# Longformer attention and a softplus feed-forward on one core: the first two batches rounded in GpSimd's transfers, and a new order

## The chip, the core and the metric

The kernel runs on one core of a Trainium2 chip. Its engines are TensorE (PE: matmuls, with weight loads shown apart as PEld), VectorE (DVE), ScalarE (ACT), GpSimd (POOL) and SyncE (SP, which here only issues transfers). Each works through its own list of instructions in order and waits on semaphores for the others. Transfers run on 16 DMA engines and are asked for by SP, POOL or ACT. The metric is the device time of one execution in microseconds.

## The reference

```python
def _attn_ref(q, k, v, global_idx):          # q, k, v: 8 x 8 x 576 x 64, float32
    scores = scale * np.matmul(q, k.transpose(0, 1, 3, 2))
    mask = np.abs(pos[:, None] - pos[None, :]) <= 32
    mask = mask | is_global[:, None] | is_global[None, :]      # 8 global tokens
    scores = np.where(mask, scores, -1e9)
    attn = softmax(scores)
    return np.matmul(attn, v)

x = attn_out.transpose(0, 2, 1, 3).reshape(4608, 512)
h = x @ w_in                                  # 512 x 2048
g = np.maximum(h, 0.0) + np.log1p(np.exp(-np.abs(h)))
return g @ w_out                              # 2048 x 512
```

So eight batches of eight heads are attended to in a window of 32 tokens on each side and eight global tokens, and every token then passes a feed-forward layer with a softplus.

## The kernel before

**Tiles.** The 576 tokens of a batch are 18 blocks of 32. A "pair" is four blocks in a row, for all eight heads; there are 36 pairs, and four pairs make a tile of 512 tokens for the feed-forward part, nine in all. A pair goes through: scores s on PE; mask, maximum m, subtraction, exponentials on ACT, sum, reciprocal rs and normalization to pn; a transposition to pt on DVE; the values xo on PE; an eviction to xT. A tile then has 64 h matmuls of 512 columns (w_in), 16 softplus evaluations on ACT (L1292) and 64 o matmuls (w_out). The first two tiles are cut into pieces of pairs (one, two, one; then one, three), so that h can begin when the first pair is through.

**First batches.** For the first two batches q and k are loaded with tokens on partitions (L512), in parts: two of 256 tokens and a short one of 64. A part is rounded to bf16 (`cast`, L837; q is scaled there), PE transposes it and picks the global tokens out of it (`tr`, L845), and the result is evicted to qx and kx (`trev`, L870). `fill` copies the global keys into kx and `gev` the global queries into qg, when all parts of k or of q are through. The global tokens' own rows come from `sg` (scores of qg against all keys), a maximum, exponentials pg, a transposition pgt, `ov` on PE, and the scaled result vg, which the first tile's values need. Later batches are loaded by blocks (L460) and rounded on POOL or ACT.

**Weights and queues.** SP loads q and k; POOL asks for v of the first batch, for w_in (four quarters, each of three transfers, L1347) and for w_out, since those transfers round on the way. `follow` (L753) is a copy of two elements on SP that reads a weight: it stops SP until the weight has landed. So the second batch's q and k follow w_in's third quarter, and its v follows w_out's first.

**Order.** All work is entered as jobs with costs in ns, dependencies and buffers (`_Order`, L19). A table of numbers, ORDER (L359), says which job comes next and on which engine; a number is five times the job's number plus the engine. Where the planner sees PE wait, it puts in fill matmuls on idle data (L729), a share FILL of the pause; its results are not used. The costs and the transfers' queues (`settle`, L110) are the planner's own estimates.

## Time and profile before

| | |
|---|---|
| median of 3 runs | 332.98 us (332.73 to 333.11) |
| the profiled execution | 333.06 us |
| its span, first to last instruction | 331.4 us |
| PE busy | 317.9 us, 96% of the span |
| ACT, DVE, POOL busy | 231.7, 220.9 and 193.3 us |
| granted TensorE clock | 0.999 |

An engine's busy time is the time in which it works on an instruction. A timeline row gives the start, the length, the engine, the line, the operation, out<-in, the shape and the number of instructions, and in brackets how long the engine was idle before it and what released it. Releasers are inferred: of several, the last to come by the profile is named. The term "issue" means that nothing in the profile explains the pause.

### The profile page before, as it was taken

The numbers are of one execution on the slowest core, as the hardware profiler recorded it, in microseconds if no ns is written. First come the engines' busy times: TensorE is split into PE (matmuls) and PEld (weight loads), VectorE is DVE, ScalarE is ACT, GpSimd is POOL, SyncE is SP. The second block draws the span as 40 slices with busy tenths as digits, with TensorE's granted clock in tenths as the row PEclk, the third lists the DMA queues.
The fourth block names the chain that finished last, engine by engine and source line by source line (L and its number), as shares of the span: only waits on it lengthen the run. The fifth ranks groups of instructions, "written<-read, shape, count | busy, mean of one in ns | idle before, by whom it ended". The sixth has DMA issues, their size and how long they took to land.

```text
span 331.4 us, 12080 instructions
## 1 busy us (share of the span) xinstructions
PE 317.9 (96%) x5281; PEld 168.8 (51%) x5281; DVE 220.9 (67%) x387; ACT 231.7 (70%) x460; POOL 193.3 (58%) x173
## 2 busy tenths in 40 slices
PE   8778998899999999999999999999999999999995
PEld 3537874576555444544454445445544454454453
DVE  7697578786995999993895498819966890440000
ACT  5799759696897678489778947866457467925712
POOL 7865654994783596878648675496327764420000
PEclk9999999999999999999999999999999999999999
DMA  7999899898878998996994759650001112000102
GB/s 192 185 201 223 166 201 177 139 184 187 154 122 156 169 209 157 203 227 112 157 188 75 179 135 143 150 168 3 4 0 65 36 65 95 2 34 32 65 16 112
DMA packets 168860, 42.14 MB, mean 127 GB/s; under 512 B 153320, under 2 KB 165864, under 8 KB 168808
## 3 DMA queue, kind: packets, MB, share of 16 engines
q1 hardware_dynamic: 155928, 27.15, 46.0%
q0 software_dynamic: 11008, 11.08, 17.0%
q10 hardware_dynamic: 1872, 3.15, 2.5%
q8 instruction: 41, 0.67, 0.9%
q14 instruction: 11, 0.09, 0.1%
HBM read 36.71 MB, written 9.44 MB: 139 GB/s over the span
## 4 chain that ended last, share of the span: by engine, by line
PE 71%; SPq 11%; DMA 9%; ACT 4%; issue 1%; POOL 1%; DVE 1%; POOLq 0%
PE o L1297 32%; PE h L1286 29%; SPq L464 5%; PE xo L1251 4%; DMA stage<-in_q_dram 4%; SPq L469 3%; PE s L1077 3%; DMA stage<-in_k_dram 3%; ACT st L1113 2%; DMA wout<-in_moe_w_out_dram 2%; PE ov L997 1%; DMA stage<-in_v_dram 1%; SPq L518 1%; PE pick L886 1%; SPq L514 1%
## 5 line engine op out<-in xcount | busy, mean ns | idle before, releaser
L1297 PE MATMUL o<-wout,g 128*128 128x512 bf16 (+1 forms) x592 | 138.6, 374 | 0.2 <-ACT g L1292 0.2
L1286 PE MATMUL h<-xT,win 128*128 128x512 bf16 (+3 forms) x768 | 136.7, 326 | 0.8 <-DMA win<-in_moe_w_in_dram 0.8
L1292 ACT ACTIVATE g<-h 128x512 bf16<-128x512 f32 (+3 forms) x192 | 83.9, 503 | 35.0 <-PE h L1286 33.4
L1286 PEld LDWEIGHTS <-win 128*128 128x128 bf16 x768 | 66.7, 98 | 59.7 <-issue 1.1
L1132 POOL TENSOR_TENSOR pn<-st,rs 128x1024 bf16<-128x1024 f32 (+1 forms) x36 | 64.7, 1806 | 42.9 <-DVE rs L1126 38.8
L1297 PEld LDWEIGHTS <-g 128*128 128x128 bf16 x592 | 55.5, 98 | 60.6 <-ACT g L1292 1.4
L1100 POOL TENSOR_TENSOR st<-st,m 128x1024 f32<-128x1024 f32 x32 | 60.5, 1899 | 28.3 <-DVE m L1094 28.2
L1124 DVE TENSOR_REDUCE sm<-st 128x8 f32<-128x1024 f32 x32 | 38.4, 1200 | 19.0 <-ACT st L1117 18.8
L1081 DVE TENSOR_TENSOR st<-s,mask 128x512 f32<-128x512 f32 x64 | 41.3, 678 | 9.3 <-PE s L1077 9.2
L1094 DVE TENSOR_REDUCE m<-st 128x8 f32<-128x1024 f32 x32 | 38.4, 1206 | 0.4
L1117 ACT ACTIVATE st<-st 128x1024 f32<-128x1024 f32 x32 | 32.7, 1051 | 3.2 <-POOL st L1100 3.0
L1141 DVE STREAM_TRANSPOSE pt<-pn 128x512 int32<-128x512 int32 x36 | 24.6, 693 | 10.4 <-POOL pn L1132 10.2
L720 ACT COPY osb<-o 128x512 f32<-128x512 f32 (+1 forms) x27 | 15.5, 575 | 20.3 <-PE o L1297 18.7
L720 ACT CAST xT<-xo 128x512 bf16<-128x512 f32 (+3 forms) x28 | 11.5, 474 | 14.5 <-PE xo L1251 14.5
L720 POOL CAST kb<-stage 128x1152 bf16<-128x1152 f32 (+2 forms) x9 | 11.5, 1273 | 10.8 <-DMA stage<-in_q_dram 8.8
L717 POOL TENSOR_SCALAR qb<-stage 128x1152 bf16<-128x1152 f32 (+1 forms) x11 | 12.9, 1177 | 8.1 <-DMA stage<-in_q_dram 6.5
L1292 ACT ACT_TABLE_LOAD x13 | 16.7, 1283 | 0.2
L1077 PE MATMUL s<-kx,qx 64*32 64x128 bf16 x1152 | 14.7, 220 | 1.3 <-issue 0.6
L720 DVE CAST xT<-xo 128x512 bf16<-128x512 f32 (+3 forms) x20 | 11.0, 582 | 6.5 <-PE xo L1251 6.5
L1077 PEld LDWEIGHTS <-qx 64*32 64x32 bf16 x1152 | 10.0, 90 | 10.3 <-issue 7.7
L720 POOL CAST vb<-stage 128x1152 bf16<-128x1152 f32 x9 | 10.3, 1150 | 6.8 <-DVE sm L1124 3.3
L1117 ACT ACT_TABLE_LOAD x11 | 14.1, 1283 | 0.2
(129 smaller groups left out, 301.6 us busy)
## 6 DMA issues: line engine op xcount, KB each, us to landing
stage<-in_v_dram SPq DMA_DIRECT2D x56, 144.0 KB, 4.2
stage<-in_k_dram SPq DMA_DIRECT2D x48, 144.0 KB, 4.1
stage<-in_q_dram SPq DMA_DIRECT2D x48, 144.0 KB, 3.5
out_dram<-osb POOLq DMA_DIRECT2D x24, 256.0 KB, 3.6
out_dram<-osb ACTq DMA_DIRECT2D x11, 256.0 KB, 2.0
stage<-in_q_dram SPq DMA_DIRECT2D x4, 512.0 KB, 6.5
stage<-in_k_dram SPq DMA_DIRECT2D x4, 512.0 KB, 7.4
wout<-in_moe_w_out_dram POOLq DMA_DIRECT2D x4, 512.0 KB, 7.8
```

What stands on the lines that cost most here:

```text
L720: {"ACT": nc.scalar.copy, "DVE": V.tensor_copy, "POOL": nc.gpsimd.tensor_copy}[e](out, in_)
L1077: nc.tensor.matmul(out=PS["s", n, g][quad(a), x, :], lhsT=qx[b % 2][rows(g), a, j * BL:(j + 1) * BL], rhs=kx[b % 2][rows(g), a, e0 * BL:(e ...
L1081: V.tensor_tensor(out=PS["st", n][:, h, :, :], in0=PS["s", n, h][:, :, :], in1=mask[:, h, j0:j0 + PB, :, :].rearrange("p j s i -> p j (s i ...
L1094: V.reduce_max(out=m[:], in_=flat(PS["st", n], h0, h1), axis=AX)
L1100: on(e).tensor_tensor(out=t, in0=t, in1=over(PS["m", n, y][:], SL * BL), op=OP.subtract)
L1117: nc.scalar.activation(out=t, in_=t, func=AF.Exp)
L1124: V.reduce_sum(out=sm[:], in_=flat(PS["st", n], h0, h1), axis=AX)
L1132: on(e).tensor_tensor(out=PS["pn", n][:, :, :, h0:h1].rearrange("p x s h -> p h x s"), in0=PS["st", n][:, h0:h1], in1=PS["rs", n, y][:].re ...
L1141: V.transpose(out=bass.AP(base.tensor, base.offset, ap=[list(base.ap[0]), [2 * STEP, PB // 2], [STEP + BL // 2, 2], [1, SL * BL]]), in_=PS ...
L1286: nc.tensor.matmul(out=h[:, :], lhsT=w_in_t[c // 4][:, kd, c % 4 * P:(c % 4 + 1) * P], rhs=PS["xT", m][:, kd, lo:hi], start=(kd == 0), sto ...
L1292: nc.scalar.activation(out=PS["g", m, c][:, lo:hi], in_=PS[key][:, lo_of(c, hi - lo)], func=AF.Softplus)
L1297: nc.tensor.matmul(out=PS["o", m, ns, a][:, :], lhsT=PS["g", m, kf][:, ns * P:(ns + 1) * P], rhs=w_out_t[kf // 4][:, kf % 4, a:z], start=( ...
```

## The change

What it does:

- The first batch's k and the second batch's q and k are no longer loaded as float32 and rounded by an engine: GpSimd's transfers write them rounded into qb and kb (`CASTS`). The second batch's v goes straight to vb as the first one's does (`VCAST`). Each 256-token part is two transfers now, of the even and of the odd tokens. Where q is rounded so, the scale is applied at the eviction of the transposed part. SP has only the first batch's q left to load of these.
- SP stops at a two-element copy out of kb, the second of k's transfers, between q's first part and the rest of q. The second batch's loads follow w_in on POOL, and the third batch's loads on SP follow w_out's last piece.
- The order of heads in a part is the natural one, and the short part of 64 tokens stands on 64 partitions for all heads, in the space of v's stage. `sg` for these batches is 16 matmuls of half the rows, not 8.
- Four k transfers stand ahead of the large count and the triangle on POOL (`make_counts`). The mask's constant (`make_neg`) may go to DVE.
- w_in's last two quarters are one tile and three transfers.
- FILL is 0.8 for 0.55, the planner's estimates of the queues differ, and ORDER was searched anew.

The core of the diff (of ORDER, some 70 lines of numbers, no row is shown):

```diff
-    FILL, FILLT, NARROW, NFILL, NFILLT = 0.55, 220, 0, 0.8, 140
+    FILL, FILLT, NARROW, NFILL, NFILLT = 0.8, 220, 0, 0.8, 140
...
+    VCAST = 2
+    CASTS = ((0, 1), (1, 1), (1, 0))
...
+    def load_part(b, w, t, e=0):
+        if t == FULL:
+            cast_ = (b, w) in CASTS
+            (nc.gpsimd if cast_ else nc.sync).dma_start(
+                out=(rounded(w, t, 0) if cast_ else natural(w, t)).rearrange("p (h d) -> p h d", d=D),
+                in_=SRC[w][b, :, FULL * NTOK:, :].rearrange("h s d -> s h d"))
+        elif (b, w) in CASTS:
+            nc.gpsimd.dma_start(out=rounded(w, t, e).rearrange("p (h d) -> p h d", d=D),
+                                in_=SRC[w][b, :, t * NTOK:(t + 1) * NTOK, :].rearrange("h (p e) d -> e p h d", e=2)[e])
+        else:
             nc.sync.dma_start(out=flat(stage[w])[:, t * 2 * HD:(t + 1) * 2 * HD].rearrange("p (h x) -> p h x", h=H),
...
-    w_in_t = [wts.tile([P, KD, WC], BF16, tag=f"win{i}", name=f"win{i}") for i in range(4)]
+    w_in_t = [wts.tile([P, KD, WC], BF16, tag=f"win{i}", name=f"win{i}") for i in range(2)]
+    w_in_x = wts.tile([P, KD, 2 * WC], BF16, tag="winx", name="winx")
...
     def add_parts(b):
...
+                if (b, w) in CASTS:
+                    was = had(("tr", 0, w, t, e)) if b else []
+                    last[0] = T["part", b, w, t, e] = o.add({"POOL": (720, 0)}, lambda eng, w=w, t=t, e=e: load_part(b, w, t, e), [last[0], *was, *(had(("w_in", 3)) if b else [])],
+                                                            rank=0, moves=1000 if t < FULL else 600, late=300)
...
+                    def emit(eng, x=x, w=w, t=t):
+                        if b:
+                            follow(0, w_in_t[2])
+                        elif t:
+                            follow(2, rounded(1, 0, 1).unsqueeze(1))
+                        load_part(b, w, t)
...
+            give = scaled if (b, w) in CASTS and not w else copy
...
+    setup("make_counts", lambda e: make_counts(), pool(1150), [], rank=-2)
```

How the rows move. First SP, from the program's start. Before (stage_60 is q's stage, stage_61 k's, stage_62 v's; trail is the two-element copy):

```order
L523 DMA gi<-in_global_idx_dram 128x16
L514 DMA stage_60<-in_q_dram 128x8x128
L514 DMA stage_61<-in_k_dram 128x8x128 x2
L518 DMA stage_61<-in_k_dram 64x4x64 x2
L514 DMA stage_60<-in_q_dram 128x8x128
L518 DMA stage_60<-in_q_dram 64x4x64 x2
L757 DMA trail<-win_126 1x2x1
```

and now:

```order
L535 DMA gi<-in_global_idx_dram 128x16
L530 DMA stage_60<-in_q_dram 128x8x128
L772 DMA trail<-kb 1x2x1
L523 DMA stage_62<-in_q_dram 64x8x64
L530 DMA stage_60<-in_q_dram 128x8x128
L772 DMA trail<-wout_126 1x2x1
```

k is gone from SP, and the copy out of kb stands ahead of q's short part and its second 256 tokens.

Second POOL, after the constants. Before:

```order
L530 IOTA pt__89 64x1 x2
L530 IOTA pos 128x448
L546 MEMSET lower 128x64
L547 AFFINE_SELECT lower<-lower 128x64
L657 MEMSET mask 128x9x32 x4
L717 TENSOR_SCALAR qb<-stage_60 128x2x4x64
L469 DMA vb_66<-in_v_dram 32x18x64 x8
L1370 COPY seen<-stage_60 128x1
L1350 DMA win_124<-in_moe_w_in_dram 128x2x512
```

and now (the TENSOR_SCALAR rounds q's short part):

```order
L527 DMA kb<-in_k_dram 128x8x64 x4
L542 IOTA pos 128x448
L559 MEMSET lower 128x64
L560 AFFINE_SELECT lower<-lower 128x64
L523 DMA stage_62<-in_k_dram 64x8x64
L1384 DMA win_120<-in_moe_w_in_dram 128x2x512
L732 TENSOR_SCALAR stage_62<-stage_62 64x512
L477 DMA vb_66<-in_v_dram 32x18x64 x2
L1387 DMA win_120<-in_moe_w_in_dram 64x2x512 x2
```

k's transfers stand ahead of the counts, and the rounding of q's short part ahead of v and of the rest of w_in.

Third DVE, at the first row maxima. Before:

```order
L639 TENSOR_SCALAR mask<-near 128x2x9x8 x2
L720 COPY qx_68<-tr 128x4x128 x2
L715 TENSOR_SCALAR qb<-stage_60 128x2x4x64
L720 CAST kx_70<-pick 128x40x8
L720 COPY kx_70<-tr 128x4x64
L1092 TENSOR_REDUCE m<-s 128x4 x3
```

and now:

```order
L652 TENSOR_SCALAR mask<-near 128x2x9x8 x2
L735 CAST qg_72<-pick 128x2x8 x2
L735 COPY kx_70<-tr 128x4x4x32
L735 CAST kx_70<-pick 128x40x8
L735 COPY kx_70<-tr 128x4x64
L1125 TENSOR_REDUCE m<-s 128x4 x3
```

The global queries qg, which are picked out of all parts of q, were evicted after the first maxima, and stand ahead of the fill of kx and of the maxima now. On ACT, too, the roundings of q's second part and the evictions of qx stand ahead of the first exponential now.

182 lines of the change are left out of this document (95 added, 87 removed), and 144 rows, old and new, of the table ORDER.

## The prediction

> **What bounds the kernel now.** First the page's head, then a table of busy time by stretches of the span (time and length, then PE, its weight loads, DVE, ACT, POOL, granted clock, DMA share, GB/s).
>
> ```profile
> span 331.4 us, 12080 instructions
> PE 317.9 (96%) x5281; PEld 168.8 (51%) x5281; DVE 220.9 (67%) x387; ACT 231.7 (70%) x460; POOL 193.3 (58%) x173
> ```
>
> ```profile
> 26.00:27.60 1.60, 0.82 (x30) 0.36 (x18) 0.85 (x4) 1.60 (x11) 1.60 (x2) 1.00 0.99 131
> 27.60:40.00 12.40, 12.36 (x276) 11.12 (x275) 8.24 (x15) 10.23 (x38) 7.60 (x16) 1.00 0.91 217
> 40.00:53.00 13.00, 11.05 (x319) 8.18 (x319) 10.33 (x15) 8.68 (x31) 6.75 (x5) 1.00 1.20 190
> 53.00:64.00 11.00, 10.93 (x137) 5.51 (x130) 8.70 (x15) 7.98 (x11) 7.69 (x5) 1.00 0.96 154
> 64.00:70.00 6.00, 4.97 (x167) 3.64 (x167) 5.18 (x10) 5.58 (x14) 5.74 (x5) 1.00 1.01 161
> 70.00:120.00 50.00, 50.00 (x943) 27.25 (x929) 41.37 (x69) 39.01 (x74) 32.17 (x24) 1.00 0.88 166
> 120.00:300.00 180.00, 179.81 (x2931) 88.49 (x2930) 125.56 (x197) 125.41 (x192) 112.08 (x77) 1.00 0.51 106
> ```
>
> From 70 us to 300 us TensorE is idle for 0.19 us of 230. From 27.6 to 70 it is idle for 0.04 + 1.95 + 0.07 + 1.03 = 3.09 us. Before 27.6 it has no matmul of the feed-forward part to do. So the change, which acts on the first two batches, can move the end in two ways only: by the moment of the first h matmul, and by how much of the 3.09 us goes or grows. All that is left after is a fixed amount of matmul work.
>
> What sets the first h matmul, from the timeline (start, length, engine, line, operation; in brackets the idle time before and its releaser):
>
> ```profile
> 14.96 0.35 ACT L1113 ACTIVATE st<-s,m 128x128 f32<-128x128 f32 x1
> 17.70 0.76 ACT L720 COPY qx<-tr 128x512 bf16<-128x512 bf16 x1
> 18.27 0.42 ACT L1113 ACTIVATE st<-s,m 128x128 f32<-128x128 f32 x1
> 19.65 0.45 ACT L720 COPY qx<-tr 128x256 bf16<-128x256 bf16 x1
> 19.90 0.47 ACT L1113 ACTIVATE st<-s,m 128x128 f32<-128x128 f32 x1
> 25.31 0.38 ACT L1008 ACTIVATE vg<-ov,grs 128x128 bf16<-128x128 f32 x1
> 26.93 0.65 ACT L720 CAST xT<-xo 128x128 bf16<-128x128 f32 x3
> 27.63 2.84 PE L1286 MATMUL h<-xT,win 128*128 128x128 bf16 x48 [0.81 <-DMA win<-in_moe_w_in_dram]
> ```
>
> ACT starts its exponentials at 14.96 us and then runs without a real pause to the scaling of the global values at 25.31 and the last eviction to xT, which ends at 27.58; h follows 0.05 us later. The row names a DMA of w_in, but the end of xT is the closer releaser. First exponential to first h is 27.63 - 14.96 = 12.67 us. Two evictions of q lie inside it; by the next ACT start they cost 0.57 and 0.25 us.
>
> **The start: what is moved.** The first batch's k leaves SP and goes to five transfers of GpSimd's queue that round on the way. SP then stops at a two-element copy out of kb until the second of them has landed, and only then asks for the rest of q and its second 256 tokens. The rows for their prices (the last three are of the table of DMA issues: KB each, us from issue to landing):
>
> ```profile
> 1.27 0.42 SPq L514 DMA_DIRECT2D stage<-in_q_dram  x1
> 5.55 0.63 ACT L713 ACTIVATE qb<-stage 128x512 bf16<-128x512 f32 x1 [0.66 <-DMA stage<-in_q_dram]
> 6.11 0.60 SPq L514 DMA_DIRECT2D stage<-in_q_dram  x1
> 11.97 0.43 DVE L715 TENSOR_SCALAR qb<-stage 128x512 bf16<-128x512 f32 x1 [0.78 <-DMA stage<-in_q_dram]
> 1.92 0.44 POOL L530 IOTA pt__89<- 128x4 f32 x3
> 6.20 5.53 POOL L469 DMA_DIRECT2D vb<-in_v_dram  x8
> 25.02 0.73 SPq L757 DMA_DIRECT2D trail<-win  x1
> win<-in_moe_w_in_dram POOLq DMA_DIRECT2D x4, 256.0 KB, 6.6
> win<-in_moe_w_in_dram POOLq DMA_DIRECT2D x1, 128.0 KB, 3.8
> vb<-in_v_dram POOLq DMA_DIRECT2D x8, 72.0 KB, 6.3
> ```
>
> GpSimd's small counts end at 2.36 us with three of them, at about 2.2 with two. A rounding transfer costs it 5.53 / 8 = 0.69 us, so the second of k is issued at 2.9. No row shows this shape; the nearest land after 3.8 us (a late w_in piece on quiet queues) and 6.3 us (v behind SP's loads). q's first load still shares the engines, so I take the middle, 5.05: landed at 7.95. SP's small copy, 0.73: 8.7. The rest of q, 0.60: 9.3. The second part of q from there to landed: the first part took 5.55 - 1.27 = 4.28 us on near-empty queues, this same load 11.97 - 6.11 = 5.86 on full ones. The queues will have drained while SP waited, so 4.28: **q's second part at 13.6 us, 1.6 us later than now.** The bounds are 2.9 + 3.8 + 0.73 + 0.60 + 4.28 = 12.3 and 2.9 + 6.3 + 0.73 + 0.60 + 5.86 = 16.4.
>
> Now this load is not on the path to the first exponential; the rows of the order say that it will be. Between that load and the first row maximum stand:
>
> ```profile
> 7.34 1.14 ACT L720 CAST kb<-stage 128x512 bf16<-128x512 f32 x2 [1.16 <-DMA stage<-in_k_dram]
> 8.67 0.38 PE L857 MATMUL tr<-ident,qb 128*128 128x128 bf16 x4
> 8.89 0.24 PE L863 MATMUL pick<-hot,qb 128*128 128x8 bf16 x4
> 18.75 0.38 DVE L720 CAST qg<-pick 64x32 bf16<-64x32 f32 x2
> 12.48 0.73 ACT L720 COPY kx<-tr 128x512 bf16<-128x512 bf16 x1
> 12.31 0.48 DVE L720 CAST kx<-pick 128x320 bf16<-128x320 f32 x1
> 13.27 0.41 PE L1077 MATMUL s<-kx,qx 64*32 64x128 bf16 x31 [0.20 <-ACT kx L720]
> 13.77 1.29 DVE L1092 TENSOR_REDUCE m<-s 128x4 f32<-128x512 f32 x2 [0.77 <-PE s L1077]
> ```
>
> Two roundings of that shape on ACT 1.14, the last transpose and pick 0.46 (8.67 to 9.13), and then on DVE in its new order qg 0.38, an eviction of k at 0.73, the fill of kx 0.48; the scores 0.41, the maximum 1.29 / 2 = 0.65. That is 4.25, with the hand-overs 4.3: first exponential at 13.6 + 4.3 = 17.9 us, against 14.96. From there 12.67 less the two evictions, which now stand ahead of it (0.57 + 0.25): 11.85. **First h at 29.75, 2.1 us later.** The bounds of the load give 28.45 and 32.5.
>
> w_in must be there too. GpSimd now rounds the rest of q between w_in's first piece and v, so v and the other eight w_in transfers queue behind that load, which lands at about 8.7 + 4.28 = 13.0. With 0.6 for the rounding and 16 transfers at 0.66, the last is issued at 24.2 and lands 3.8 to 6.6 us later, at 28.0 to 30.8. The first h in the new order reads the joined piece, which is this last one; it agrees with 29.75 and does not allow much less. So a gain at the start is nearly excluded, though k itself needs no rounding any more: the 1.14 us of ACT above, once more for its second part, and that work waits for q all the same. The counts behind k come 2.8 us later (four transfers at 0.69); what DVE makes of them is due at the first scores, which come three us later too.
>
> Edits at no price: the fills. The clock is granted at 1.00 in each stretch above, so there is nothing to win; they stand where PE waits, the sixteen ahead of the third scores for banks that ACT holds for eight exponentials, 2.8 us; they hold PE 3.8 us (0.059 for 128 columns by the h row, 0.24 for a fill's 512), and with the mask matmuls and scores behind them the third maximum is still there before ACT has done sixteen. The joined w_in piece is one issue less of each kind, at the end of a queue that ends in time. Eight more sg matmuls in the second batch (0.43 for eight, in a row below) against eight transposes and eight picks fewer in its two short parts: between 0 and +0.4, taken as +0.2. The searched order also moves rows after 70 us; there is no idle time to win there, and a loss is in the range.
>
> **Behind the first h.** Where the 3.09 us of idle time lie:
>
> ```profile
> 40.36 0.25 PE L1077 MATMUL s<-kx,qx 64*32 64x128 bf16 x8 [0.38 <-DVE kx L720]
> 47.16 0.68 PE L1077 MATMUL s<-kx,qx 64*32 64x128 bf16 x56 [0.58 <-issue]
> 52.81 0.43 PE L968 MATMUL sg<-kx,qg 128*32 128x320 bf16 x8 [1.00 <-issue]
> 64.67 0.22 PE L1251 MATMUL xo<-pt,vg 32*64 32x64 bf16 x4 [0.40 <-ACT osb L720]
> 65.24 0.21 PE L1251 MATMUL xo<-pt,vg 32*64 32x64 bf16 x2 [0.35 <-ACT g L1292]
> ```
>
> 0.38 us waits for the second batch's k, 1.03 us from 64 to 70 for the next tile's probabilities and global values, and 1.58 us are called issue: PE waits for nothing that the profile shows. The second batch now asks through GpSimd right after w_in and its first normalizations, with ten roundings and both of v's gone from ACT, DVE and POOL. Its chain is nearer to ready when PE, which comes 2 us later, gets there; I take the 0.38 and the 1.03 as gone. Of the issue pauses, which follow long runs of small matmuls, I take half: 0.8. Saved: about 2.2 us, with bounds of 3.09 and, if the denser run of transposes and scores pauses PE more, -1.
>
> **Sum.** +2.1 + 0.2 - 2.2 = +0.1 us. The profiled execution took 333.06 us, 1.66 around its span; the median of the runs is 0.08 lower. So 333.06 + 0.1 - 0.08 = 333.1, no change that can be measured: this kernel's runs lie within 0.38 us of each other, and I call 0.2%, 0.67 us, the least that tells.
>
> **Rivals.** One: q pays in full, slower. k lands like v did, after 6.3 us; SP stands until 9.2, q's second part lands at 14.8, first exponential 19.1, first h 31.0: +3.3, and +0.2. The issue pauses stay, so 1.4 are saved: +2.1, 335.1. It decides from about 14.2 us for that load on. For it: v took 6.3 although it was issued early. Against it: SP's loads were then in front of it, and now only one is.
>
> Two: faster. The load lands at 12.3 as by the low bound, w_in binds at 28.9, +1.3, and nothing of the idle time stays: +1.3 + 0.2 - 3.1 = -1.6, 331.4. For it: less copying on three engines in the stretch where all the idle time lies. Against it: the pauses called issue have nothing to do with copying.
> [...]
>
> Three: the transfers of k are not issued at their price, because DVE fills and copies at the same moment. Eight of v took 0.69 each while DVE was busy too, so stretching is not in the trace; if the first two each waited for one DVE fill of 0.48 us, q would come 1.0 us later: +1.1, 334.1.
> [...]
>
> **Chances.** Forecast 0.43, own range 332.0 to 334.1; faster 0.31; q in full 0.23; stretched issues 0.03. The range for 8 in 10 goes from 330.7, near the faster rival with idle time gone and w_in early, to 335.3. Of the forecast's own cases a fifth lie beyond 0.67 us on either side: faster 0.31 + 0.08 = 0.39; slower 0.26 + 0.08 = 0.34; same 0.27.
>
> **What would show it.** q's second part rounded at 13 to 14.5 us and SP's small copy at 7.5 to 8.5; first exponential at 17 to 18.5 with DVE's qg ahead of the fill; first h at 29 to 30.5; PE idle for 0.5 to 1.5 us between there and 70, and hardly after. A first h below 28.4, or idle time above 3 us behind it, makes the forecast wrong.

## The result, and the profile after

The changed kernel takes 342.88 us (median of 4 runs, 342.11 to 344.09) against 332.86 us (332.59 to 333.11) for the kernel before in the same series. The ratio is 1.0305, with a 95% interval of 1.0273 to 1.0336: about 10 us slower, where I had forecast no change. The profiled execution took 342.8 us. In what follows, ratios come from undisturbed runs alone; the kept traces of e5, e9 and e14 are of disturbed executions, so no whole time is read from them, and nothing at all from e9's.

The head of the page after, and the same kind of table by stretches as ahead of the prediction (time and length, then PE, its weight loads, DVE, ACT, POOL, granted clock, DMA share, GB/s):

```profile
span 341.1 us, 12063 instructions
PE 326.0 (96%) x5288; PEld 174.3 (51%) x5288; DVE 224.0 (66%) x397; ACT 224.3 (66%) x444; POOL 209.4 (61%) x185
```

```profile
33.20:43.00 9.80, 9.41 (x228) 8.53 (x227) 6.28 (x14) 9.14 (x39) 9.80 (x17) 1.00 1.65 122
43.00:56.00 13.00, 10.65 (x279) 8.57 (x277) 8.06 (x13) 5.88 (x22) 10.80 (x13) 1.00 1.47 173
56.00:68.00 12.00, 11.83 (x197) 7.10 (x196) 11.70 (x19) 9.76 (x20) 9.05 (x6) 1.00 1.29 148
68.00:80.00 12.00, 10.11 (x245) 6.11 (x244) 11.54 (x23) 8.57 (x18) 7.87 (x6) 1.00 0.95 165
120.00:300.00 180.00, 178.91 (x2879) 87.79 (x2877) 128.87 (x205) 126.49 (x195) 122.21 (x86) 1.00 0.54 111
```

From the first h at 33.20 to 80 us PE is idle for 0.39 + 2.35 + 0.17 + 1.89 = 4.80 us, where it was 3.09. From 120 to 300 it is 1.09, where it was 0.19. The score matmuls take 1.7 us more (below); 0.6 of that lies ahead of the first h. With the 5.57 us by which the first h is later, this makes 5.57 + 1.71 + 0.90 + 1.1 = 9.3 of the 9.7 us by which the span grew. The largest piece lies in front of the first h, which the timeline shows (start, length, engine, line, operation, in brackets the idle time before and its releaser):

```profile
7.91 0.73 SPq L772 DMA_DIRECT2D trail<-kb  x1
7.92 0.72 POOL L1384 DMA_DIRECT2D win<-in_moe_w_in_dram  x1
9.46 0.62 SPq L530 DMA_DIRECT2D stage<-in_q_dram  x1
14.21 0.61 POOL L732 TENSOR_SCALAR stage<-stage 64x512 bf16<-64x512 f32 x1 [5.58 <-DMA stage<-in_q_dram]
14.88 0.29 PE L886 MATMUL tr<-ident,stage 64*128 64x64 bf16 x4 [3.44 <-POOL stage L732]
15.18 2.13 PE L744 MATMUL warm<-vb 128*128 128x512 bf16 x7
15.46 1.15 ACT L728 ACTIVATE qb<-stage 128x512 bf16<-128x512 f32 x2 [2.86 <-DMA stage<-in_q_dram]
21.82 0.37 ACT L1146 ACTIVATE st<-s,m 128x128 f32<-128x128 f32 x1 [0.88 <-DVE m L1125]
25.36 1.22 POOL L1387 DMA_DIRECT2D winx<-in_moe_w_in_dram  x2 [1.34 <-DMA win<-in_moe_w_in_dram]
33.20 0.82 PE L1319 MATMUL h<-xT,winx 128*128 128x128 bf16 x8
```

SP's small copy goes out at 7.91 us, as forecast (7.95). But q's second part lands at 15.46 and not at 13.6, the first exponential starts at 21.82 and not at 17.9, and the first h at 33.20 and not at 29.75: 5.57 us later than before. From exponential to h it is 11.38 us; I had said 11.85.

A second chain ends at the same place. POOL stands 5.58 us for the rest of q, and only behind its rounding does it ask for v and for the rest of w_in; after another 1.34 us of waiting the last two transfers of w_in go out, the very last at 25.96. It lands 7.4 us later, at 33.4. By the single starts in the trace the first two h matmuls run at 33.20 and 33.25 and the third at 33.52, when this landing has released it. So two chains ended within 0.3 us of each other: q's, and w_in's.

Between 15.46 and 21.82 something stands that the prediction did not have. PE's clock in the table by stretches of 1 us (the 1.00, 0.64 and 0.50 behind the bracketed counts):

```profile
15.00:16.00 1.00, 1.00 (x12) 0.56 (x11) 0.00 (x0) 0.55 (x2) 1.00 (x2) 1.00 0.00 0
16.00:17.00 1.00, 1.00 (x5) 0.38 (x3) 0.00 (x0) 0.86 (x3) 1.00 (x3) 0.64 1.15 74
18.00:19.00 1.00, 1.00 (x19) 0.98 (x18) 0.41 (x3) 0.00 (x0) 1.00 (x3) 0.50 1.11 122
```

After 3.44 us without a matmul PE runs at a granted clock of 0.50 from 16.28 to 19.69 us, with seven fills (2.13 us) in front of q's transposes.

### The profile page after: what moved, and what is told of

Its sections match the earlier page's. It is cut to its first block, busy times and chain, and to the rows that moved or that the text cites. A ratio compares the mean times of both kernels' runs of the same rounds, so it can differ in the third digit from the quotient of the medians.

```text
span 341.1 us, 12063 instructions
## 1 busy us (share of the span) xinstructions
PE 326.0 (96%) x5288; PEld 174.3 (51%) x5288; DVE 224.0 (66%) x397; ACT 224.3 (66%) x444; POOL 209.4 (61%) x185
## 4 chain that ended last, share of the span: by engine, by line
PE 82%; DVE 7%; ACT 4%; DMA 3%; issue 1%; POOL 1%; SPq 0%; POOLq 0%
PE h L1319 35%; PE o L1330 33%; PE xo L1284 4%; PE s L1110 4%; ACT st L1146 2%; DMA stage<-in_q_dram 2%; DMA kb<-in_k_dram 1%; PE tr L886 1%; DVE sm L1157 1%; PE ov L1032 1%; DVE pick L606 1%; PE pick L908 1%; DVE st L1114 1%; PE warm L744 1%; DVE pt L1174 1%
## 5 line engine op out<-in xcount | busy, mean ns | idle before, releaser
L1165 POOL TENSOR_TENSOR pn<-st,rs 128x1024 bf16<-128x1024 f32 (+1 forms) x37 | 65.7, 1788 | 29.6 <-DVE rs L1159 26.5
L1319 PE MATMUL h<-xT,winx 128*128 128x512 bf16 (+3 forms) x384 | 75.4, 326 | 1.4 <-issue 1.2
L1319 PE MATMUL h<-xT,win 128*128 128x512 bf16 (+3 forms) x384 | 71.8, 326 | 2.0 <-DVE xT L735 1.9
L1319 PEld LDWEIGHTS <-win 128*128 128x128 bf16 x384 | 33.3, 98 | 32.9 <-DVE xT L735 2.4
L1319 PEld LDWEIGHTS <-winx 128*128 128x128 bf16 x384 | 33.7, 98 | 30.5 <-issue 0.7
L735 ACT COPY osb<-o 128x512 f32<-128x512 f32 (+1 forms) x26 | 14.8, 571 | 19.9 <-PE o L1330 19.5
L735 DVE CAST xT<-xo 128x512 bf16<-128x512 f32 (+3 forms) x21 | 11.2, 575 | 10.3 <-PE xo L1284 10.2
L744 PE MATMUL warm<-vb 128*128 128x512 bf16 x60 | 16.8, 436 | 1.3 <-DVE vb L564 1.3
L735 POOL CAST kb<-stage 128x1152 bf16<-128x1152 f32 x8 | 11.9, 1502 | 9.3 <-DMA stage<-in_v_dram 5.1
L1110 PE MATMUL s<-kx,qx 64*32 64x128 bf16 x1152 | 16.4, 219 | 0.7 <-issue 0.7
```

Source lines behind the costliest of these rows:

```text
L735: {"ACT": nc.scalar.copy, "DVE": V.tensor_copy, "POOL": nc.gpsimd.tensor_copy}[e](out, in_)
L1110: nc.tensor.matmul(out=PS["s", n, h][quad(c), x, :], lhsT=qx[b % 2][rows(g), a, j * BL:(j + 1) * BL], rhs=kx[b % 2][rows(g), a, e0 * BL:(e ...
L1165: on(e).tensor_tensor(out=PS["pn", n][:, :, :, h0:h1].rearrange("p x s h -> p h x s"), in0=PS["st", n][:, h0:h1], in1=PS["rs", n, y][:].re ...
L1319: nc.tensor.matmul(out=h[:, :], lhsT=w_in_t[c // 4][:, kd, c % 4 * P:(c % 4 + 1) * P], rhs=PS["xT", m][:, kd, lo:hi], start=(kd == 0), sto ...
```

## The experiments

All times are medians of single runs; the ratios, with 95% intervals, are to the kernel before on the same chip. The edits are to the changed kernel unless something else is said; its order by numbers stays as it is.

**The stop alone: e1_no_stop.**

```
-                        elif t:
-                            follow(2, rounded(1, 0, 1).unsqueeze(1))
```

> The changed kernel without SP's stop: the small copy out of kb ahead of q's later parts is left out, so SP issues the rest of q and its second part at once behind the first. Theory 'late q': the stop alone carries most of the 5.57 us by which the first h matmul came later (27.63 to 33.20). Then q's second part lands by 10 us instead of 15.46, PE has no pause over 2 us before 16, the granted clock stays at 1.00 there, the first exponential starts at 14.5 to 16 (21.82 with the stop), the first h at 26 to 28, and the time is 335 to 337.5 us. Rival 'shared transfers': without the stop q's packets take k's time; k's pieces land 2 us later or more, the first exponential stays above 18, and the time stays above 339.

Measured: 340.98 us, ratio 1.0217 (1.0176 to 1.0258). q came in time, PE's pause was gone, and still the first exponential started only at 20.56. PE's timeline and clock of this run:

```profile
9.98 0.40 PE L884 MATMUL tr<-ident,kb 128*128 128x128 bf16 x4 [0.59 <-DMA kb<-in_k_dram]
10.90 0.40 PE L884 MATMUL tr<-ident,kb 128*128 128x128 bf16 x4 [0.44 <-DMA kb<-in_k_dram]
12.24 1.66 PE L744 MATMUL warm<-vb 128*128 128x512 bf16 x4
14.24 2.48 PE L744 MATMUL warm<-vb 128*128 128x512 bf16 x7
```

```profile
9.00:12.00 3.00, 1.45 (x29) 1.18 (x27) 2.76 (x12) 2.65 (x5) 2.85 (x5) 1.00 2.27 164
13.00:14.00 1.00, 1.00 (x7) 0.17 (x5) 0.69 (x3) 0.41 (x1) 1.00 (x2) 0.50 2.06 169
```

k's second piece, whose landing let SP go on at 7.91 us in the changed kernel, is now waited for until 10.90, with q's loads under way beside it (the rival "shared transfers" was right in that). PE waits for k in three short pieces, 0.59, 0.44 and 0.52 us. In those 3 us it is busy for 1.45. Behind them the granted clock was 0.50, by the table from about 12.5 to 15.9 us, and the eleven fills, which wait for nothing but PE, took 1.66 + 2.48 = 4.1 us of the path. So the stop is a part of the loss, not most of it; the theory "late q" alone falls. The stop had also held w_in: without it POOL rounds q's rest at 8.66 and not at 14.21, the last w_in transfer goes out at 20.91 and not at 25.96, and no h waits for it (first h at 31.94).

**The fills and the clock: e3_no_fill and e4_fill_pause.** Both set the number of fills ahead of chosen pieces of work (59: transposes of q's rest, 62: those of q's second part). The planner's routine for fills looks the piece up first:

```
+    OWN = {62: 0}                  # e4: {59: 16, 62: 0}
-        count = int((t1 - t0) * share / step)
+        count = self.OWN.get(n_, int((t1 - t0) * share / step))
```

> The changed kernel without the seven fills that stand between the transposes of the rest of q and those of q's second part; SP's stop stays. Theory 'late q': the fills only hold PE from 15.18 to 17.31, while both roundings are ready at 16.6: the transposes start 0.7 to 1.1 us earlier, the first exponential at 20.7 to 21.2, the time 341.6 to 342.3. Rival 'the fills keep the clock': without them the granted clock stays at 0.50 longer and takes the gain back, 342.6 to 343.5.

> The changed kernel with twelve more fills ahead of the transposes of the rest of q, where PE stood for 3.44 us, and without the seven behind them; SP's stop stays. It prices the clock apart from the lateness. Theory 'cold clock': with the pause under 1 us the granted clock stays at 1.00 up to 20 us, the way from q's landing (15.46) to the first exponential takes the 4.3 us that I forecast instead of 6.36, so the first exponential starts at 19.6 to 20.2, the first h at 31.0 to 31.6, and the time is 340.5 to 341.2. Rival 'only the order': the clock was not what made it long; the first exponential starts at 20.8 or later and the time is above 341.5.

Measured: 343.24 us, ratio 1.0285 (1.0245 to 1.0324), and 344.54 us, ratio 1.0333 (1.0296 to 1.037). Neither helps. Without the seven fills the granted clock was 0.58 in the stretch from 15 to 16 us and 0.50 from there to 22, and the first exponential came at 22.73, later than with them by 0.91 (0.33 of it by q's landing): the rival "the fills keep the clock" was right. With twelve more fills the pause of 3.44 us was filled at a granted clock of 1.00, and then came another:

```profile
10.32 3.61 PE L748 MATMUL warm<-vb 128*128 128x512 bf16 x16
16.08 0.61 PE L890 MATMUL tr<-ident,qb 128*128 128x128 bf16 x4 [1.57 <-ACT qb L732]
21.18 0.37 ACT L1150 ACTIVATE st<-s,m 128x128 f32<-128x128 f32 x1 [1.32 <-DVE m L1129]
34.57 0.50 PE L1323 MATMUL h<-xT,winx 128*128 128x128 bf16 x6 [1.75 <-DMA winx<-in_moe_w_in_dram]
```

```profile
17.00:18.00 1.00, 1.00 (x20) 0.98 (x18) 0.47 (x3) 0.00 (x0) 1.00 (x3) 0.50 1.13 157
```

Behind these 1.57 us of waiting for ACT's rounding the granted clock was 0.50 from about 16.1 to 19.5 us, for as long as behind the 3.44. The run therefore does not price the clock by itself as I had meant it to: it moved the pause and did not remove it. And what it gained it could not keep: the first exponential came 0.64 us earlier and the first h 0.66 us earlier (32.54), but then PE stood 1.75 us for the last of w_in, and the third h ran at 34.57, later than the changed kernel's 33.52. In the kept trace of every run with the stop the third h is released by this landing (33.52 to 36.98). With the stop in place, no repair of the clock or of q's second part alone could have brought h into flow sooner.

**Both together: e6_no_stop_fills.** The stop goes as in the first run, and the fills go where PE waits for k:

```
+    OWN = {48: 2, 50: 2, 52: 2, 59: 0, 62: 0}
```

> The changed kernel without SP's stop, and with the eleven fills that stand ahead of the rest of q and of q's second part taken away; two fills each stand ahead of k's first, second and third transposes instead, where PE waited 0.59, 0.44 and 0.52 us for k's transfers in the run without the stop. In that run q came in time, but the three short waits in a row were followed by a granted clock of 0.50 from 12.7 to 16.1 us, and the eleven fills took 4.1 us on the path. Theory 'clock and fills': with PE kept busy the clock stays at 1.00, q's second part is transposed by 14, the first exponential starts at 16.5 to 17.8 (20.56 without the stop alone), the first h at 27.8 to 29.3, and the time is 336.5 to 338.5 us (340.98 without the stop alone). Rival 'k late': k's fourth piece or its rest lands so late that the first exponential stays above 19 and the time above 339.5.

Measured: 337.17 us, ratio 1.0117 (1.0074 to 1.0159), in the forecast of the theory "clock and fills". The granted clock is 1.00 in every stretch up to 300 us, and PE is busy for 2.66 of the 3 us in which it had 1.45:

```profile
9.00:12.00 3.00, 2.66 (x31) 1.19 (x29) 2.76 (x11) 2.75 (x5) 2.83 (x5) 1.00 2.19 167
```

```profile
17.37 0.37 ACT L1148 ACTIVATE st<-s,m 128x128 f32<-128x128 f32 x1 [0.83 <-DVE m L1127]
30.89 0.50 PE L1321 MATMUL h<-xT,winx 128*128 128x128 bf16 x6 [1.88 <-DMA winx<-in_moe_w_in_dram]
71.17 1.58 PE L1321 MATMUL h<-xT,win 128*128 128x128 bf16 x24 [2.21 <-DVE xT L739]
```

The first exponential is at 17.37 and the first h at 28.73. What comes to the front then are two waits: 1.88 us for the last of w_in, and 2.21 us for a copy to xT on DVE, which stood in the changed kernel too. Not all of the gain is the clock's: against e1 the first exponential is 3.2 us earlier, but the third h only 1.2 (30.89 against 32.05). Most of the rest lies between 43 and 56 us, where PE idles for 0.50 us and not for 2.90, 1.71 of them a pause called issue.

**How long q's load takes: e14_win_behind.** Back to the changed kernel with its stop. Number 78 is the step that issues w_in's first 256 KB.

```
-  ... 212, 28, 78, 227, 39, 293, ...   ... 337, 43, 83, 48, ...
+  ... 212, 28, 227, 39, 293, ...       ... 337, 43, 78, 83, 48, ...
```

> The changed kernel with its stop, but w_in's first transfer (256 KB, issued by POOL at 7.92, ahead of q's later parts) goes behind the rounding of q's rest and v's first two transfers. Theory 'shared transfer': q's second part took 6.0 us from issue to landing, where I had reckoned 4.28, because w_in's packets ran beside it; without them it lands at 14.0 to 14.7 in place of 15.46 (its own spread over the profiles so far is 14.87 to 16.3). Rival 'it takes that long': it lands at 15 to 16 as before. The time moves little either way (341.5 to 344.5), since w_in then lands later too.

Measured: ratio 1.0257 (1.0203 to 1.0311). The rows of its trace:

```profile
9.37 0.62 SPq L530 DMA_DIRECT2D stage<-in_q_dram  x1
13.51 1.15 ACT L728 ACTIVATE qb<-stage 128x512 bf16<-128x512 f32 x2 [1.77 <-DMA stage<-in_q_dram]
14.71 0.40 PE L886 MATMUL tr<-ident,qb 128*128 128x128 bf16 x4 [0.22 <-ACT qb L728]
18.71 0.37 ACT L1146 ACTIVATE st<-s,m 128x128 f32<-128x128 f32 x1 [0.84 <-DVE m L1125]
36.30 0.80 PE L1319 MATMUL h<-xT,winx 128*128 128x128 bf16 x6 [2.73 <-DMA winx<-in_moe_w_in_dram]
```

Without w_in's packets beside it, q's second part takes 13.51 - 9.37 = 4.14 us, against 15.46 - 9.46 = 6.00 with them. My 4.28 and 13.6 were the numbers of this kernel, not of the changed one. "Shared transfer" holds, and behind PE's pause here, 1.92 us, the granted clock was 1.00 from 12 to 21 us. The time hardly gains: w_in is later still, and the third h waits for it until 36.30.

**The score matmuls: e2_banks and e5_tiles.** The busy time of the 1152 score matmuls rose from 14.7 us (the group's row of the kernel before) to 16.4. My first theory was the bank that they write.

```
+    def turns(b):
+        if b < EARLY:
+            return [(2 * h + c // 2, c % 2, c, h) for x in range(2) for y in range(2) for h in range(2) for c in [2 * y + (h ^ x)]]
+        return heads(b)
-                for a, g, c, h in heads(b):
+                for a, g, c, h in turns(b):
```

> The changed kernel, but the 32-row score matmuls of the first two batches are written in an order in which one goes to the bank of h 0 and the next to the bank of h 1, as the kernel before does; the changed kernel writes all four of h 0 and then all four of h 1. Nothing else moves. Theory 'same bank': a run of matmuls that all write one bank is slower, 0.63 us for 32 of them against 0.42; then the group of 32 falls back to 0.42, the busy time of the s matmuls from 16.4 to 14.7 us, and the time falls by 1.0 to 1.8 us, to 341.0 to 341.9. Rival: the pace comes from the operands (the halves of the array that they sit in), 0.63 stays and the time is 342.5 to 343.2.

Measured: 344.37 us, ratio 1.0298 (1.0257 to 1.0339). The groups' rows (busy us, mean ns of one, then idle before them) of the kernel before, of the changed kernel and of this run say that nothing got faster:

```profile
L1077 PE MATMUL s<-kx,qx 64*32 64x128 bf16 x1152 | 14.7, 220 | 1.3 <-issue 0.6 <-DVE kx L720 0.4 <-ACT kx L720 0.2
```

```profile
L1110 PE MATMUL s<-kx,qx 64*32 64x128 bf16 x1152 | 16.4, 219 | 0.7 <-issue 0.7
```

```profile
L1115 PE MATMUL s<-kx,qx 64*32 64x128 bf16 x1152 | 16.6, 219 | 0.6 <-issue 0.6
```

The theory falls. The starts of the single matmuls in the trace, in ns from the first of a set of 32 (sets without a pause), showed why:

```
before, first batches:  0 3 6 10 13 16 20 23 | 55 70 73 76 80 83 86 89 | ...     from first to last: 198 to 202
changed, first batches: 0 3 7 10 | 66 69 72 76 | 122 125 128 132 | 177 ...        from first to last: 411
banks alternating:      0 4 7 10 | 66 70 73 76 | 122 125 129 132 | 178 ...        from first to last: 411
changed, later batches: 0 4 7 10 14 17 20 24 | 66 70 73 76 80 83 86 90 | ...      from first to last: 201
```

Eight matmuls of 64 rows by 32 columns start within 24 ns in one case and four within 10 ns in the other. With the heads in their natural order a head's row half is c % 2 and its quarter of the columns is c: each quarter meets only one half of the rows, and of the eight parts, each a half with a quarter, four are used, whatever the order or the bank. The next run gives the first two batches the pairing of the later ones:

```
-        if b < EARLY:
-            return [(2 * h + c // 2, c % 2, c, h) for h in range(2) for c in range(R)]
         return [(a ^ g, g, a ^ g, g) for a in range(HG) for g in range(2)]
```

(and the same pairing where the global scores and their copies are written).

> The changed kernel, but in the first two batches the score matmuls and the global ones use the pairing of row half and quarter of columns that the later batches use (h equal to the row half, the quarter equal to the column group), in place of the one that the natural order of heads gives. It leaves the outputs of the first two batches in the wrong heads; the work is the same in number and size. The starts of the single matmuls in the trace show groups of four that start together every 56 ns in the first two batches of the changed kernel and of the run with alternating banks, and groups of eight in the later batches and in the kernel before: with the natural order each quarter of columns meets only one half of the rows, so four of the eight parts of the array are used. Theory 'four of eight parts': with the other pairing 32 of them take 0.20 us from first to last start instead of 0.41, the busy time of the s matmuls falls from 16.4 to 14.7 us or less, and the time by 1.0 to 2.0 us against the changed kernel. Rival 'the bank' is out by the run before; rival 'hidden': PE waits elsewhere for as long, and the time moves by less than 0.5 us.

Measured: 342.51 us, ratio 1.0255 (1.0201 to 1.0309). Its group's row:

```profile
L1102 PE MATMUL s<-kx,qx 64*32 64x128 bf16 x1152 | 14.8, 221 | 0.1
```

The size is shown: with all eight parts in use the group takes 1.6 us less of PE's time. That it is 1.6 us of the kernel's time is not shown: the interval of the ratio overlaps that of the changed kernel. The work is not quite the same in number: with this pairing there are 64 sg matmuls in place of 80, 5.5 us of PE's time in place of 5.9.

**Behind the first h: e8_subs and e9_pick_late.** Two theories on PE's wait of 1.89 us ahead of 76.21.

```
e8:  -  ... 783, 1933, 1938, 1943, 1773, 1728, 1948, ...
     +  ... 783, 1773, 1728, 1933, 1938, 1943, 1948, ...
e9 (on top of e6):  197 (DVE builds pick) goes from behind 1986 to behind 1837
```

> The changed kernel with the subtractions of the fourth and fifth pair written on POOL ahead of the second batch's four v transfers and not behind the third of them, where they now wait until 51.50 for a transfer that waits for w_out. Theory 'POOL behind w_out': the subtractions start at 45 to 46 (44.92 in the kernel before), what follows on POOL comes 3 to 5 us earlier, PE's idle time between 43 and 80 falls from 4.4 to about 3 us, the wait of 1.89 us ahead of 76.21 is gone, and the time falls by 1.2 to 2.0 us. Rival 'not POOL': PE's waits there come from DVE or ACT and stay, and the time moves by less than 0.5 us, or v is late and it becomes longer.

Measured: 343.79 us, ratio 1.0295 (1.026 to 1.0331). The subtractions went ahead of v, and then waited as long for DVE:

```profile
51.22 3.75 POOL L1133 TENSOR_TENSOR st<-st,m 128x1024 f32<-128x1024 f32 x2 [4.82 <-DVE m L1127]
```

So POOL's wait for w_out, which I had taken for a cause, cost nothing that shows. What PE's wait does end in is DVE's queue. The rows of the changed kernel, and the one of the kernel before that answers to the first of them:

```profile
71.52 3.71 DVE L606 TENSOR_TENSOR pick<-posK,gf 32x144 bf16<-32x144 f32 x4
75.90 0.45 DVE L735 CAST xT<-xo 128x128 bf16<-128x128 f32 x2
76.21 1.58 PE L1319 MATMUL h<-xT,win 128*128 128x128 bf16 x24 [1.89 <-DVE xT L735]
```

```profile
74.20 1.24 DVE L593 TENSOR_TENSOR pick<-posK,gf 32x144 bf16<-32x144 f32 x4
```

The four operations took 3.71 us where they had taken 1.24, and the new order has them in front of the transposes and copies that h waits for. The first two, 1.61 and 1.45 us long, run beside a normalization and a rounding of k on POOL and end 0.15 and 0.10 us behind them (72.98 and 74.50). The last two, with POOL free of such work, take 0.30 each, as all four do in the kernel before. In e6, again with a normalization and a rounding on POOL beside the first of them, the four take 3.69. So the long ones go with POOL's work beside them; that this work is the cause was not tried.

> The kernel of the run without the stop and with the fills moved (337.17 us), with one thing more: the step that builds pick for the third batch on DVE (65.06 to 70.2 there; it stood at 73.4 in the kernel before) goes behind the copies to xT and the transposes that the third part of the values and h wait for. In that run PE waits 2.21 us ahead of 71.17 for DVE's xT, and the same wait stands ahead of 76.21 in the changed kernel (1.89). Theory 'pick in front on DVE': this wait falls below 0.5 us and the time by 1.5 to 2.2 us, to 335.0 to 335.7. Rival 'POOL's subtractions' (already without gain when they were moved alone): DVE waits for POOL's pn there anyway, the wait stays above 1.5 us and the time above 336.7.

Measured: 335.74 us, ratio 1.0061 (1.0031 to 1.0091), as the theory "pick in front on DVE" says. In the trace of e13 below, which has the edit in it, this wait is 0.45 us (ahead of 72.21). The step from e6, 0.0056 of the ratio, is just outside what the two intervals allow for chance (0.0052).

**What lies on w_in: e10_h_order and e11_winx_split,** both on top of e6.

```
e10: h and softplus of columns 8-11 -> 0-3, 0-3 -> 4-7, 4-7 -> 8-11, in the order's numbers
e11: +        if x == 2:
     +            for u in range(2):
     +                weights_part(w_in_x[:, :, u * WC:(u + 1) * WC], moe_w_in[:, (x + u) * WC:(x + u + 1) * WC], y)
```

> The kernel of the run without the stop and with the fills moved, with one thing more: the first h matmuls go through the columns 0 to 3, 4 to 7 and then 8 to 11 of w_in's blocks (with their softplus in the same order) where the searched order takes 8 to 11 first, which lie in w_in's last pieces. PE waits there 1.88 us, until 30.89, for the last piece. Theory 'last pieces first': the first h matmuls run at 28.7, six to eight of them ahead of the wait, the wait falls to about 1 us or less, and the time falls by 0.7 to 1.9 us. Rival 'hidden': what follows waits for the last pieces by as much, and the time moves by less than 0.4 us.

> The kernel of the run without the stop and with the fills moved, with one part of the change undone: w_in's last pieces go out again as two halves of 512 columns each (the same steps, twice the transfers). In that run they took 8.3 and 8.6 us from issue to landing, at 134 to 180 GB/s from 21 to 27 us, where the kernel before moved 200 GB/s with its smaller pieces. Theory 'one piece is slow': they land 1 to 2 us earlier, PE's wait until 30.89 falls by as much, and the time by 0.8 to 1.8 us. Rival 'POOL': the two to three more issues of 0.6 to 0.75 us each delay POOL by 1.9 us and the landing stays at 30 to 31.5; the time moves by less than 0.5 us or becomes longer.

Measured: 337.46 us, ratio 1.0105 (1.0059 to 1.0151), and 337.97 us, ratio 1.0121 (1.0062 to 1.0179), against e6's 1.0117. No gain in either. Yet in both traces the wait for w_in is gone (in e11 h runs on from 28.70 without one), so the theories were right on the wait and wrong on the time. Other pauses came up: in e11 1.96 us called issue and two stretches at half clock of about 3.4 us each (a mean of 0.89 from 45 to 60 and of 0.91 from 60 to 80 us), in e10 these two:

```profile
26.54 1.24 PE L748 MATMUL warm<-vb 128*128 128x512 bf16 x5 [1.00 <-ACT st L1148]
48.67 0.56 PE L1321 MATMUL h<-xT,win 128*128 128x128 bf16 x7 [0.98 <-issue]
```

**All eight parts, without and with more transposes: e13_pick_tiles and e12_all.** e13 is e9 with the pairing of e5. e12 is e9 with e10's order and the pairing made good for the results: each head is transposed by itself into the row half that the later batches give it.

```
-                nc.tensor.transpose(out=ps[:, e, a, 0:n], in_=x[:, a * P:(a + 1) * P], identity=ident[0:n, 0:n])
+                for g in range(2):
+                    nc.tensor.transpose(out=ps[rows(g), e, a, 0:n], in_=x[:, rows(HG * g + a)], identity=ident[0:n, 0:n])
```

> The kernel of the run without the stop and with the fills moved, with pick behind, with the h matmuls in the other order, and with all eight parts of the array in the first two batches: the transposes take one head at a time (64 columns) and write it to the row half that the later batches give it, so the heads are where they belong. If the prices add up: 337.17 less 1.5 to 2.2 (pick), less 0.7 to 1.9 (h), less 1.0 to 1.9 (eight parts), plus up to 0.5 for twice as many transposes: 331.5 to 334.3 us, about the 332.86 of the kernel before or below it. If they hide one another, the time stays above 335.

> The kernel with pick behind (no stop, fills moved; 335.7 us), with the pairing of row half and column quarter of the later batches in the first two batches' scores, and with the transposes as they are, so that no matmul is added. It leaves the outputs of the first two batches in the wrong heads; the work is the same in number and size. The run with all changes together took twice as many transposes for the pairing and was slower, with 2.6 us of PE's waits ahead of the s matmuls that end in issue. Theory 'eight parts': 32 scores take 0.42 us in place of 0.63, and the time falls by 1.0 to 1.9 us to 333.8 to 334.7, most of what still lies between this kernel and the 332.9 to 333.4 of the kernel before. Rival 'hidden': PE waits elsewhere for what it saves, mostly in issue, and the time stays at 335.2 or above.

Measured: e12 has a ratio of 1.0232 (1.0143 to 1.0321), about 341 us, and e13 335.45 us, ratio 1.006 (1.0033 to 1.0086). The groups' rows of e12, then of e13:

```profile
L1106 PE MATMUL s<-kx,qx 64*32 64x128 bf16 x1152 | 15.1, 220 | 2.9 <-issue 2.6 <-ACT kx L737 0.2
```

```profile
L1104 PE MATMUL s<-kx,qx 64*32 64x128 bf16 x1152 | 14.6, 220 | 0.3 <-ACT kx L737 0.2
```

In e12 the saved time comes back as pauses of PE that end in nothing but issue. Twice as many small instructions stand in front of the scores; what the traces show of such pauses is in the last section. In e13 the scores take 14.6 us and the kernel is no faster than e9: "hidden" is right by its range, though a gain below some 1.3 us could not be told from chance here. Three rows of its timeline, and the stretch in which the wait for xT stood:

```profile
22.53 0.76 PE L1026 MATMUL ov<-vb,pgt 32*32 32x129 bf16 x40 [1.27 <-DVE pgt L1016]
29.47 0.50 PE L1313 MATMUL h<-xT,winx 128*128 128x128 bf16 x6 [0.80 <-DMA winx<-in_moe_w_in_dram]
48.33 0.38 PE L1313 MATMUL h<-xT,winx 128*128 128x128 bf16 x4 [1.00 <-issue]
```

```profile
60.00:80.00 20.00, 18.97 (x444) 12.43 (x448) 14.85 (x31) 16.25 (x44) 12.15 (x8) 1.00 0.91 152
```

From 60 to 80 us PE is idle for 1.03 us, part of which is four matmul records that this trace lacks (444 beside 448 weight loads); e6 has 2.21 in one wait there. What the scores save is waited off elsewhere: 1.27 us for DVE's pgt, which was 0.78 in e6, and 1.00 in issue.

**The account.** By the ratios, times 333 us, the 10.2 us of the change fall into: the stop 2.9 (1.0305 to 1.0217), the place of the fills, with the clock and the later pauses that changed with it, 3.3 (to 1.0117), pick in front of the copies on DVE 1.9 (to 1.0061), and 2.0 that stay. The intervals are some 1.0 to 1.4 us wide to either side, so these are sizes, not decimals. The first two are not independent: without the stop the clock still fell, and with the stop no arrangement of fills that I tried kept it, and w_in would have held h in any case. The 2.0 us that stay fit the first h of e13 (28.39, in full flow from 29.47, against 27.63): there 0.80 is the wait for w_in, and the first exponential is 2.07 later (17.03 against 14.96). But taking the wait for w_in out of e6 gained nothing, so what the 2.0 us hang on is open. No version beat the kernel before.

## Why the prediction was wrong

**"All that is left after is a fixed amount of matmul work", and from exponential to h 11.85.** The second is right, 11.38. The first nearly: 0.9 us more idle time from 120 to 300, and an amount of work that was not fixed (the scores, below).

**SP's stop, 7.95.** Right at 7.91, but by luck, since two errors cancelled: a transfer of k costs POOL 0.97 us and not 0.69 (four took 3.87), and lands sooner after its issue than the middle that I took (4.7 us by the table of DMA issues, not 5.05). Rival three had this stretched issue, and put it down to DVE's fills. Six transfers of this shape for the second batch, at 30.50 to 35.85 us, took 0.88 to 0.94 each, and the one at 39.37 took 0.94 with no DVE instruction beside it, so the traces do not show DVE as the cause.

**"The queues will have drained while SP waited, so 4.28."** This is the first step that failed. I had w_in's first piece on the list of POOL's work ahead of v, and did not put it on the queue beside q. It went out at 7.92, q's second part at 9.46, and the load took 6.00 us. Moved away, it took 4.14 (e14). My upper bound for this term, 5.86, was nearly the truth. It also passes the 14.2 us from which I let the rival "q in full" decide. That rival had the outcome, q's second part later than 14.2, but another reason, a late k, with the same 4.28 for the load; and at 335.1 it had a fraction of the price.

**"Load to first exponential 4.3."** It took 6.36. In e14, at a granted clock of 1.00, it took 18.71 - 13.51 = 5.20, so 0.9 was left out by me: on PE the transposes of two more pieces of k and the mask matmuls stand between q's transposes and the first scores, and the scores take 0.63 us or more instead of 0.41. The other 1.2 are the clock and the seven fills.

**"Edits at no price: the fills."** The second step that failed. I read the granted clock of 1.00 in every stretch as a property of the kernel. It was what that order of the work had been granted: my own forecast left PE without transposes from about 11 to 14 us, and I priced that pause as waiting time only. I looked at the sixteen fills ahead of the third scores and not at the seven ahead of q's transposes.
In the changed kernel PE stood for 3.44 us there, and behind it 0.64, 0.50, 0.50 and 0.66 from 16 to 20 us make (0.36 + 0.50 + 0.50 + 0.34) / 0.5 = 3.4 us at half pace. PE was not idle for all of the 3.41 us ahead of the fall: from 12.86 to 16.28 it was busy for 0.41 of the time (see the last section).

**w_in "at 28.0 to 30.8".** The third step that failed: the mechanism was right, each of its terms too small. q's rest was rounded at 14.21 and not at 13.0, the last transfer was issued at 25.96 and not at 24.2, with 1.34 us of POOL's own waiting in between, and it took 7.4 us, above my 3.8 to 6.6. So w_in was complete at 33.4, and the third h waited for it until 33.52. The bound was reached in the changed kernel, 2.6 us above my highest value, and it would have kept h from full flow even if q's second part and the clock had come as forecast. In e6 it binds until 30.89.

**"Saved: about 2.2 us" behind the first h.** The idle time grew by 1.7, beyond my bound of -1. Of the pieces that I counted on, the wait for k shrank only from 0.38 to 0.28, the 1.03 between 64 and 70 did go, and of 1.58 in issue 1.16 + 0.17 are left (I took half of it as gone without a mechanism). What I had no term for is work that the searched order puts in front: pick on DVE (1.89, shown by e9), and q's second-batch transposes behind DVE and ACT (0.91 and 0.29 us ahead of 47.40 and 48.62).

**"Eight more sg matmuls, +0.2."** The natural order of heads changed more than the number of matmuls. The diff shows the pairing (2h + c/2, c % 2, c, h); I read it as a new order of the same work, and did not ask which row half meets which columns. It costs 1.6 to 1.8 us of PE's time (16.4 against 14.8 in e5 and 14.6 in e13); that it costs the kernel as much is not shown.

The forecast named two signs that would make it wrong; the second, idle time above 3 us behind the first h, is what came (4.80 up to 80 us), beside a first exponential and a first h later than any that I had listed.

## What to carry to other kernels

When a change makes TensorE wait for a load that was hidden, price the wait twice: as waiting time, and as a stretch at half clock behind it, which here was 3.4 us long and cost 1.7 us of PE's work; the clock of 1.00 in the profile before said nothing about a gap that was not yet there. Fills worked in front of the pieces that wait (e6); between a landing and the work that it releases they stood in the path (e1), though taking them away alone did not help (e3). For every load that becomes critical, list what the other queues have issued in the 2 us before it and which loads are asked for only behind it, as w_in was here. When one chain has been repaired, look at where the next one ends before you put a price on the repair. For every row that moves to another place in the order, ask what is queued behind it there.

## What was not expected of the hardware

- The granted clock fell behind less than 3.4 us without work, and not by the length of the pause alone. In e1 PE was busy for 1.45 of 3 us with three pauses of 0.59, 0.44 and 0.52, and in e4 it paused once for 1.57 us; behind both the clock was 0.50 for about 3.4 us. Behind pauses of 1.51 us (e10, ahead of 13.59) and 1.92 us (e14, ahead of 12.51) it was 1.00. The wait for xT was 2.22 us in e8 (ahead of 76.57) and 2.21 in e6 (ahead of 71.17): the clock was 0.50 behind the first, from about 77.6 to 81.0 us, and 1.00 behind the second. Nor does PE's busy share of the 3.41 us ahead decide alone: it was 0.41 ahead of the fall in the changed kernel, 0.55 in e1 and 0.48 in e4, but 0.45 in the changed kernel from 74.30 to 77.71, with a clock of 1.00 behind it. What decides is open.
- One such stretch, 3.41 us at 0.50, is 1.7 us of PE's work, 0.5% of this span. The changed kernel's four runs had a mean clock of 0.994 with 342.1 and 342.8 us, and of 0.990 with 343.0 and 344.1. The wait for xT is one place where a second stretch can stand, as in e8:

```profile
78.00:79.00 1.00, 1.00 (x38) 0.67 (x36) 1.00 (x1) 0.35 (x1) 0.00 (x0) 0.50 1.26 205
```

- Score matmuls of the same shape, 64 by 32, and of the same mean duration (220 and 219 ns) started eight within 24 ns and the next eight 55 to 66 ns behind the first of them in the first batches of the kernel before, and four within 10 ns and the next four 56 to 66 ns behind the first in the changed kernel's first batches. What e5 and e13 changed was the pairing of row half and column quarter, and the group's busy time went from 16.4 to 14.8 and 14.6 us.
- The pauses called issue ended shortly behind a packet of one DMA queue, which the page calls instruction (packets, MB, share; the share was 0.9% in the kernel before, with as many packets and MB):

```profile
q8 instruction: 41, 0.67, 0.8%
```

The two kernels' traces have four pauses of PE of 0.4 us or more that end in issue. Those until 47.16 and 52.81 in the kernel before (0.58 and 1.00 us) end 1.34 and 1.37 us behind the landing of such a packet, those until 53.43 and 141.96 in the changed kernel (1.16 and 0.73 us) 1.45 and 1.53 us behind one. What the packets hold, whether they cause the pauses, and why most of the 41 go without one is open.
